# Three more pairs by seven products, ten stages' diagonal tiles on ScalarE, and a new order of steps

## The chip, the cores and the metric

The kernel runs on one core of a Trainium2 chip. Its time is the device time of one execution in microseconds (us), as the median of several runs. Five engines work side by side, each with its own queue in order: TensorE (PE, with its weight loads shown as PEld), VectorE (DVE), ScalarE (ACT), GpSimd (POOL) and SyncE (SP), which here only issues transfers.

## The reference

Two operations follow each other: a recurrent attention with a decaying state, and a two-layer network with a leaky activation.

```python
batch, n_heads, seq, head_dim = (4, 8, 768, 48)
for t in range(S):
    cur = np.einsum('bhd,bhe->bhde', u[None] * kt, vt)
    y[:, :, t] = np.einsum('bhd,bhde->bhe', rt, state + cur)
    state = w[None, :, :, None] * state + np.einsum('bhd,bhe->bhde', kt, vt)
...
n_tokens, d_model, d_ff = (3072, 384, 2048)
h = x @ w_in
g = np.maximum(0.01 * h, h)
return (g @ w_out).astype(np.float32)
```

The inputs are float32, the output is float32 of 3072 x 384.

## The kernel before

**Stages and pairs.** The 4 x 768 tokens are cut into 24 stages of 128 tokens, numbered n = 0 to 23; six stages make one sequence, so stages 0, 6, 12 and 18 start from an empty state. Two stages make a pair, m = 0 to 11, and the network works on pairs. The work of the attention inside a stage is done in chunk form: scaled queries and keys, a 128 x 128 product per head, a mask, and a state that is carried to the next stage.

**The list of steps.** The order of all work is one string, ORDER (L25 to L27). Each word is a step with its stage or pair; the program goes through the words, and each step appends its instructions to the queues of the engines it uses. Nothing is reordered afterwards, so the list sets the order in every queue at once. An instruction waits, by semaphores that `Sched.resolve` finds, for whatever wrote its inputs or still reads its target. The words:

- k, r, v and a number: load that stage's keys, queries or values by a transfer that POOL issues; wi and wo load a quarter of the weights each, also by POOL. Keys and queries lie in 14 buffers.
- P: scale queries and keys (VectorE, one instruction, or two where the word has no ".1" and n < 4). For n >= 8 the step also lets SP issue a transposing transfer, qk to tp.
- T: for n < 8 the transpose by TensorE, with two evictions on ScalarE. X: for n < 6 a product on VectorE for the diagonal.
- A: the 128 x 128 products of a stage, in two PSUM banks. M: mask and evict them into the tile `at` (VectorE).
- K: products of keys and values for the state. S: the state's update (VectorE).
- Q: for n < 6 one product on VectorE; for later stages three VectorE instructions that give `s_tok`, one number per token and head, and then `diag_tile` (L351), which fills `at` with a diagonal matrix for each head. M later writes the masked products over it, leaving the diagonal.
- Y: the output of the attention, with an eviction to xT on ScalarE.
- G (a stage, a quarter of the first layer) and J (a pair, an eighth of it): products into one bank, with the activation on ScalarE into gT.
- H (a stage): the second layer, 16 products of 384 columns, an eviction on ScalarE, and a store that SP issues.
- V, B and Z: the second layer of a pair by seven products of half size in place of eight. V (four steps, once) forms sums of weight blocks in `tw`, B (four steps a pair) sums of blocks of gT in `gs`, both on VectorE. Z (seven steps a pair) has 8 products of 192 columns each; ScalarE copies a partial sum to `snap`, or VectorE adds one, and the finished half of a row block is stored.
- U, C, W: small tables. F: filler products without a result. I: skip so many PSUM banks.

Every step that needs a bank takes the next of eight in turn (`next_bank`), so a step waits for the reader of the step that had the bank before; I lets the turn pass banks that a Z sequence still holds.

**Before the change** Z is used for the pairs 8 to 11 and H for the stages 0 to 15. All diagonal tiles of stages 6 to 23 are made by POOL, two instructions of 128 x 512 each, in the queue that also issues all loads. In `g2_seven`, `store` writes out a row block of 128 x 384 when its second half has landed; the last pair alone stores each half by itself.

## Time and profile before

| | |
|---|---|
| median of 3 runs | 169.43 us (169.15 to 169.71) |
| the profiled execution | 169.63 us, span 167.8 us |
| granted TensorE clock, mean | 1.00 |
| instructions | 5041 |
| loads and stores in HBM | 20.45 MB read, 4.72 MB written |

The span is the part of an execution that the trace covers, from its first to its last event. In the rows of the trace "PE" is the product, "PEld" its weight load; "L561" is the line of the kernel; out<-in names the tiles. A row of a group has its count, the busy time, the mean of one in ns, the idle time of the engine just before, and what ended it. A row of the timeline starts with the start and the length in us. A row of the stretches has the stretch, its length, the busy time of each engine with its count of instructions, the granted clock, the transfer engines' share and GB/s.

### The profile page before, as it was taken

To read this page: it belongs to the slowest core of one execution; us is meant where nothing else is said; L and a number is where in the kernel's file an instruction comes from. 1 tells how busy PE (TensorE), PEld (TensorE's weight loads), DVE (VectorE), ACT (ScalarE), POOL (GpSimd) and SP (SyncE) were. 2 spreads that over 40 slices of the span, in tenths; PEclk is the share of its full clock that TensorE was granted. 3 is DMA by queue.
4 is the path that set the end of the run, shared out by engine and by line. 5 is a ranking of instruction groups with operands and counts; after the bars stand their busy time and mean duration, and the time that the engine had idled before them with its cause. 6 is when DMAs were issued, how large, how long until landed. Compare 5 with 4: busy or idle time off the path is not lost.

```text
span 167.8 us, 5041 instructions
## 1 busy us (share of the span) xinstructions
PE 159.4 (95%) x2166; PEld 126.3 (75%) x2166; DVE 117.8 (70%) x205; ACT 94.2 (56%) x179; POOL 107.0 (64%) x119
## 2 busy tenths in 40 slices
PE   6697899999999999999899999999999999999993
PEld 2265698898566769955778887766699889999992
DVE  7399987927605979989898499935899396313571
ACT  4766678798223448821549783521288787485310
POOL 7999999999999899797999963750044200000000
PEclk9999999999999999999999999999999999999999
DMA  5999999999999999999999997512125000110224
GB/s 99 120 132 144 170 180 164 184 205 149 148 159 198 168 142 149 223 132 132 169 145 132 108 141 120 117 47 95 49 71 108 0 4 0 47 51 0 78 69 141
DMA packets 100090, 19.67 MB, mean 117 GB/s; under 512 B 93154, under 2 KB 100068, under 8 KB 100068
## 3 DMA queue, kind: packets, MB, share of 16 engines
q0 software_dynamic: 76512, 10.03, 95.5%
q1 hardware_dynamic: 22514, 9.12, 27.2%
q8 instruction: 17, 0.28, 0.7%
q10 hardware_dynamic: 1042, 0.20, 0.6%
q14 instruction: 5, 0.04, 0.1%
HBM read 20.45 MB, written 4.72 MB: 150 GB/s over the span
## 4 chain that ended last, share of the span: by engine, by line
PE 81%; DMA 9%; POOL 7%; issue 1%; DVE 0%; ACT 0%; POOLq 0%; DVEq 0%; ACTq 0%
PE ps_all L561 32%; PE ps_all L578 22%; PE ps_all L650 11%; PE ps_all L544 6%; POOL rk_sb L213 5%; DMA tp<-qk 5%; PE ps_all L511 4%; DMA w_in_sb<-in_moe_w_in_dram 4%; PE ps_all L388 3%; POOL v_sb L213 2%; PE ps_all L438 2%; PE ps_all L368 1%; PE ps_all L516 0%; POOL w_in_sb L228 0%; DVE at L398 0%
## 5 line engine op out<-in xcount | busy, mean ns | idle before, releaser
L561 PE MATMUL ps_all<-xT,w_in_sb 128*128 128x256 bf16 x480 | 57.0, 273 | 0.0
L567 ACT ACTIVATE gT<-ps_all 128x512 bf16<-128x512 f32 x80 | 47.8, 597 | 12.9 <-PE ps_all L561 9.3
L355 POOL TENSOR_TENSOR at<-ident,s_tok 128x512 bf16<-128x512 bf16 x36 | 39.3, 1119 | 23.0 <-DVE s_tok L347 22.9
L561 PEld LDWEIGHTS ps_all<-xT,w_in_sb 128*128 128x128 bf16 x480 | 45.8, 98 | 6.1
L578 PE MATMUL ps_all<-w_out_sb,gT 128*128 128x384 bf16 x256 | 43.5, 326 | 0.0
L578 PEld LDWEIGHTS ps_all<-w_out_sb,gT 128*128 128x128 bf16 x256 | 24.5, 98 | 15.8
L398 DVE CAST_PREDICATED at<-mask,ps_all 128x1024 bf16<-128x1024 uint16 x18 | 21.4, 1218 | 15.3 <-PE ps_all L388 15.2
L584 ACT ACTIVATE out_sb<-ps_all 128x384 f32<-128x384 f32 x16 | 7.9, 491 | 37.0 <-PE ps_all L578 37.0
L213 POOL DMA_DIRECT2D v_sb<-in_v_dram x24 | 22.5, 942 | 0.3 <-issue 0.3
L213 POOL DMA_DIRECT2D rk_sb<-in_k_dram x23 | 21.2, 929 | 0.0
L213 POOL DMA_DIRECT2D rk_sb<-in_r_dram x23 | 21.0, 923 | 0.0
L313 DVE TENSOR_TENSOR qk<-rk_sb,tab 128x768 bf16<-128x768 bf16 x23 | 16.0, 704 | 4.4 <-DMA rk_sb<-in_r_dram 4.4
L544 PE MATMUL ps_all<-xT,w_in_sb 128*128 128x128 bf16 x192 | 12.7, 219 | 0.8 <-DMA w_in_sb<-in_moe_w_in_dram 0.8
L481 DVE TENSOR_TENSOR sum_t<-ps_all,st 128x384 bf16<-128x384 f32 x14 | 7.7, 552 | 6.4 <-PE ps_all L438 6.3
L544 PEld LDWEIGHTS ps_all<-xT,w_in_sb 128*128 128x128 bf16 x192 | 11.1, 98 | 1.3 <-DVE prod L328 0.9
L345 DVE TENSOR_TENSOR ku<-rk_sb,ku 128x384 bf16<-128x384 bf16 x18 | 11.3, 628 | 0.6
L531 ACT ACTIVATE xT<-ps_all 128x384 bf16<-128x384 f32 x24 | 10.5, 493 | 2.1 <-PE ps_all L516 1.4
L549 ACT ACTIVATE gT<-ps_all 128x512 bf16<-128x512 f32 x16 | 9.6, 603 | 3.7 <-PE ps_all L544 3.4
L511 PE MATMUL ps_all<-at,v_sb 128*32 128x128 bf16 x384 | 10.5, 220 | 0.1
L347 DVE TENSOR_REDUCE s_tok<-ku 128x8 f32<-128x384 bf16 x18 | 9.9, 553 | 0.6
L375 ACT ACTIVATE tp<-ps_all 128x512 bf16<-128x512 f32 x16 | 8.7, 600 | 2.9 <-PE ps_all L368 2.9
L616 DVE TENSOR_TENSOR gs<-gT 128x1024 bf16<-128x1024 bf16 x8 | 5.4, 687 | 7.0 <-PE ps_all L650 5.3
(75 smaller groups left out, 188.3 us busy)
## 6 DMA issues: line engine op xcount, KB each, us to landing
out_dram<-out_sb SPq DMA_DIRECT2D x22, 192.0 KB, 2.6
v_sb<-in_v_dram POOLq DMA_DIRECT2D x24, 96.0 KB, 6.5
rk_sb<-in_k_dram POOLq DMA_DIRECT2D x23, 96.0 KB, 6.4
rk_sb<-in_r_dram POOLq DMA_DIRECT2D x23, 96.0 KB, 7.0
w_in_sb<-in_moe_w_in_dram POOLq DMA_DIRECT2D x4, 384.0 KB, 7.5
w_out_sb<-in_moe_w_out_dram POOLq DMA_DIRECT2D x4, 384.0 KB, 8.5
out_dram<-out_sb SPq DMA_DIRECT2D x4, 96.0 KB, 1.6
tp<-qk SPq DMA_TRANSPOSE x16, 4.4
```

Source lines behind the costliest of these rows:

```text
L213: add("pool", lambda: G.dma_start(dst, src), R=pace, W=[key], dma=f"{which}{n}")
L313: add("dve", lambda: V.tensor_tensor(qk[iq][:, :, 0:D], both, by, ALU.mult), R=[("r", n % NRK), ("k", n % NRK), "qtab", "ktab", ("qk0", iq ...
L345: add("dve", lambda: V.tensor_tensor(ku[i2][:, :], r_of(n), ku[i2][:, :], ALU.mult), R=[("r", n % NRK), ("ku", i2)], W=[("ku", i2), ("rku" ...
L355: add("pool", lambda hh=hh, s_of=s_of: G.tensor_tensor(at[ia][:, hh, :, :], ident[:, :].unsqueeze(1).to_broadcast([128, NP, 128]), s_of.un ...
L398: add("dve", lambda: V.copy_predicated(at[n % NAT][:, :, :, :].rearrange("p two m i -> p (two m) i"), mask[:, :].bitcast(mybir.dt.uint16). ...
L511: last = PE.matmul(ps_y[32 * q:32 * q + 32, 128 * s:128 * s + 128], a, m, start=first_mm and (s == 0 or n >= DIAG), stop=last_mm and n >= ...
L531: add("act", lambda: A.activation(xT[m % NX][:, :, 128 * half:128 * half + 128], ps_y[:, 0:HD].rearrange("p (s t) -> p s t", t=128), AF.Copy),
L544: last = PE.matmul(ps_g[:, 128 * f:128 * f + 128], w_in_sb[:, s, 128 * fb:128 * fb + 128], xT[ix][:, s, t], start=s == 0, stop=s == NSL - 1)
L561: last = PE.matmul(ps_g[:, 256 * f:256 * f + 256], w_in_sb[:, s, 128 * fb:128 * fb + 128], xT[ix][:, s, :], start=s == 0, stop=s == NSL - 1)
L567: add("act", lambda: A.activation(gT[ig][:, 2 * j:2 * j + 2, :].rearrange("p f t -> p (f t)"), ps_g[:, :], AF.Prelu, alpha=0.01), R=[key], ...
L578: last = PE.matmul(ps_o[:, 0:HD], gT[ig][:, s, 128 * half:128 * half + 128], w_out_sb[:, s, :], start=s == 0, stop=s == NFB - 1)
L650: done = PE.matmul(ps_o[:, 0:NH], lhs[:, s, :], rhs[:, s, :], start=first and s == 0, stop=s == HF - 1, skip_group_check=not (first and last))
```

## The change

Four edits. The list ORDER is replaced by another one with the same kinds of step (466 words in place of 434). The diagonal tiles of stages 14 to 23 are made by ScalarE, eight instructions of 128 x 128 a stage, one for each head, with that head's column of s_tok as the scale. Pairs 5, 6 and 7 join the pairs with seven products, so that H is left for the stages 0 to 9. The last two pairs store each half of a row block by itself, where only the last one did. The lists, cut to their beginnings and to a part further on that the prediction speaks of:

```diff
-v0 U k1 k2 I1 P0 r1 P1.1 r2 k3 T0 F4 C W A0 r3 X0 P2.1 wi3 T1 K0 M0.0 Q0 T2 X1 S0 P3.1 Y0 X2 A2 M2.4 T3 v1 K1 G0.3 k4 Q1 A1 r4 A3 S1 P4 v2 K2 M1.2 T4 v3 k5 Y1 X3 Q2 M3.0 wi2 S2 K3 Y2 Q3 G1.3 G1.2
...
+P0 k1 r1 I4 k3 T0 k2 r3 r2 I1 r4 P1.0 v0 I3 X0 T1 W k4 v1 U P3.1 wi3 k5 P2.1 F2 I3 A1 X1 C T3 v2 M1.0 r5 v3 wi1 P4 v4 v5 r9 I2 K0 Q0 T2 X3 A0 T4 S0 K1 M0.4 r6 k6 I4 I4 Q1 wi0 A2 A3 S1 M2.1 X2 Y1 M3.2 P5 I1 Y0 G1.3 K2 r7 k7 v6 k9 wi2 wo0 wo3 S2 G0.3 v7 K3 T5 Q2 Q3 A4 S3 wo1 wo2 X4 X5 M4.0 Y2 Y3 G1.1
...
+k14 A7 r10 G0.2 J2.2 M7 J2.4 K7 J2.5 S7 G2.2 V0 Y6 Y7 Q8 J2.0 P8 J2.6 P9 r16 r23 I4 H3 H1 H0 P11 r21 Q11 J3.0 Q10 P10 J3.5 P13 J3.4 J3.3 H2 r15 K8 k12 v12 A8 A9 J3.2 M9 r12 J3.6 M8 k16 k15 S8 H4 K9 v11 Y9 I3 Q13 v18 k19 k17 v14 S9 Y8 J3.1 K10 P14 J4.0 S10 J4.5 J4.2 J4.6 J3.7 k18 v21 r17 k21 v13 Q14 P12 r18 J4.1 A11 A10 M11 I1 Q15 Q12 J4.7 H5 H7 M10 Y11
...
+Z6.0 J7.6 Z6.1 Z6.2 Q20 B6.3 Q21 Z6.3 K19 Z6.4 P23 J8.7 J8.0 J8.3 P21 I1 Z6.5 S19 J7.2 Z6.6 A20 J8.6 J7.4
...
```

```diff
-    SEVEN = (8, 9, 10, 11)
+    AT = (14, 15, 16, 17, 18, 19, 20, 21, 22, 23,)
+    SEVEN = (5, 6, 7, 8, 9, 10, 11)
...
     def diag_tile(n, i2):
         ia = n % NAT
+        if n in AT:
+            for h in range(H):
+                add("act", lambda h=h: A.activation(at[ia][:, h % 2, h // 2, :], ident[:, :], AF.Copy,
+                                                    scale=s_tok[i2][:, h:h + 1]),
+                    R=["ident", ("s", i2)], W=[("at", ia, h % 2)])
+            return
         for hh in range(2):
...
-            if final:
+            if m >= NST // 2 - 2:
                 add("sp", lambda: SP.dma_start(out[128 * n:128 * n + 128, cols], out_sb[io][:, cols]),
                     R=[("o", io, c)], W=[("out", n, c)], dma=f"o{io}{c}")
```

## The prediction

> **What bounds the kernel now.** I read first the page's busy shares, then the busy time by stretches of the span, then the chain that ended last, and only then groups and single instructions. The page names TensorE; the stretches (stretch, its length, then busy time of PE, PEld, DVE, ACT, POOL) say since when:

> ```profile
> PE 159.4 (95%) x2166; PEld 126.3 (75%) x2166; DVE 117.8 (70%) x205; ACT 94.2 (56%) x179; POOL 107.0 (64%) x119
> 6.40:22.00 15.60, 13.70 (x234) 10.17 (x235) 12.52 (x27) 9.90 (x22) 15.60 (x19) 1.00 2.11 148
> 35.00:74.00 39.00, 39.00 (x431) 28.98 (x431) 26.96 (x41) 20.71 (x38) 37.55 (x41) 1.00 1.92 170
> 74.00:83.00 9.00, 8.47 (x180) 5.78 (x178) 8.00 (x13) 3.12 (x7) 7.94 (x10) 1.00 1.67 130
> 83.00:100.00 17.00, 17.00 (x217) 14.20 (x211) 13.77 (x20) 11.77 (x21) 15.53 (x17) 1.00 2.10 136
> 100.00:165.00 65.00, 65.00 (x829) 54.50 (x827) 42.35 (x70) 33.85 (x67) 12.37 (x11) 1.00 0.25 58
> 165.00:167.80 2.80, 0.00 (x1) 0.00 (x0) 0.00 (x0) 0.33 (x1) 0.00 (x0) 1.00 0.49 171
> ```

> From 35 us to 165 us TensorE is busy all the time but for 0.53 us. So only three things move the end: the amount of TensorE work, the idle time before about 22 us (1.9 us after the first transposes, and products that wait on loads), and the 2.8 us after the last product. Any gain on another engine is worth nothing by itself; any new wait of TensorE costs its full length.

> The chain (start, length, work) gives what a step costs when nothing holds it:

> ```profile
> 13.59 7.27 DMA w_in_sb<-in_moe_w_in_dram
> 23.27 0.45 PE ps_all L368 x8
> 30.53 1.34 PE ps_all L544 x24
> 54.48 0.17 PE ps_all L438 x4
> 59.22 0.90 PE ps_all L511 x56
> 64.95 3.93 PE ps_all L561 x36
> 74.95 7.60 DMA tp<-qk
> 85.38 2.60 PE ps_all L578 x16
> 93.46 0.33 PE ps_all L388 x8
> 152.46 12.55 PE ps_all L650 x152
> ```

> T 0.45, G 0.67 (24 products are two), K 0.17, Y 0.45 (56 are two), J 0.655 (36 are six), H 2.60, A 0.33; one of the seven products Z has 8 instructions, 12.55 / 19 = 0.66.

> **The products.** A pair by two H steps takes 5.20 us of TensorE, by seven Z steps 7 x 0.66 = 4.62. Pairs 5, 6 and 7 change over: 3 x 0.58 = **1.73 us less**. It is a full gain, since these pairs lie where TensorE never stops. What they add elsewhere, by these rows:

> ```profile
> L584 ACT ACTIVATE out_sb<-ps_all 128x384 f32<-128x384 f32 x16 | 7.9, 491 | 37.0 <-PE ps_all L578 37.0
> L398 DVE CAST_PREDICATED at<-mask,ps_all 128x1024 bf16<-128x1024 uint16 x18 | 21.4, 1218 | 15.3 <-PE ps_all L388 15.2
> L658 ACT ACTIVATE snap<-ps_all 128x192 f32<-128x192 f32 x12 | 4.0, 331 | 4.9 <-PE ps_all L650 4.6
> L616 DVE TENSOR_TENSOR gs<-gT 128x1024 bf16<-128x1024 bf16 x8 | 5.4, 687 | 7.0 <-PE ps_all L650 5.3
> L681 DVE TENSOR_TENSOR out_sb<-ps_all,snap 128x192 f32<-128x192 f32 x13 | 4.6, 357 | 5.5 <-PE ps_all L650 5.5
> ```

> VectorE gets four sums and three additions a pair, 4 x 0.687 + 3 x 0.357 = 3.8 us, 11.5 for three; ScalarE four copies of 0.331 for two of 0.491, 1.0 us in all. Hidden while the engines keep up with TensorE. The four V steps move ahead by some forty steps; their work stays the same.

> **The diagonal tiles.** For ten stages POOL loses two instructions of 1.119 us, 22.4 us in all, and ScalarE gets eight of 128 columns with a scale column. No such instruction is in the trace. The nearest are these two, with a scale column and a source in SBUF, and the one behind them:

> ```profile
> L355 POOL TENSOR_TENSOR at<-ident,s_tok 128x512 bf16<-128x512 bf16 x36 | 39.3, 1119 | 23.0 <-DVE s_tok L347 22.9
> 5.11 0.61 ACT L295 ACTIVATE tab<-lnw,qexp 128x384 bf16<-128x384 f32 x1
> 5.63 0.60 ACT L296 ACTIVATE tab<-lnw,kexp 128x384 bf16<-128x384 f32 x1
> 83.65 2.08 POOL L355 TENSOR_TENSOR at<-ident,s_tok 128x512 bf16<-128x512 bf16 x2
> 83.65 2.29 DVE L345 TENSOR_TENSOR ku<-rk_sb,ku 128x384 bf16<-128x384 bf16 x1
> 77.05 0.36 DVE L345 TENSOR_TENSOR ku<-rk_sb,ku 128x384 bf16<-128x384 bf16 x1
> ```

> They start 0.52 apart for 384 columns. From 192 to 384 columns a copy goes from 331 to 491 ns, 0.83 ns a column; 256 columns fewer take 0.21 off, so 0.31 each, between 0.31 and 0.39 (0.60 less 0.21, no overlap). I take 0.31, as eight stand in a row: 2.45 us a stage, 24.5 us for ten. ScalarE goes from 94.2 to 119.7 us, 72% of the span.

> The last three rows show what POOL's tiles cost today: VectorE's product of 0.36 us takes 2.29 while POOL multiplies. That gives some of the 11.5 us back; how much does not matter, because VectorE does not set the end after 35 us.

> What can matter is order. The new ScalarE instructions stand in its queue ahead of the evictions that free TensorE's eight banks, and the first of each eight waits for VectorE's s_tok. At its tightest, Q20 and Q21 stand together: 4.9 us, then J8.7's eviction of 0.5. Until the list takes J8.7's bank again TensorE has Z6.3, K19, Z6.4, J8.7, J8.0, J8.3, Z6.5, J7.2, Z6.6, A20, J8.6: 4 x 0.66 + 0.17 + 5 x 0.655 + 0.33 = 6.4 us. That covers it by 1.0 us, if VectorE has s_tok in time. Behind Q14, J4.1's eviction is done after 2.45 + 0.5 us and its bank is wanted after J4.1, A11, A10, J4.7 and H5, 3 x 0.66 + 2.6 = 4.6.

> **The start.** The page rows for loads and the rows that set the start:

> ```profile
> rk_sb<-in_r_dram POOLq DMA_DIRECT2D x23, 96.0 KB, 7.0
> 4.14 1.78 POOL L213 DMA_DIRECT2D rk_sb<-in_r_dram  x2
> 8.57 0.56 DVE L313 TENSOR_TENSOR qk<-rk_sb,tab 128x768 bf16<-128x768 bf16 x1 [1.72 <-DMA rk_sb<-in_r_dram]
> 13.59 0.83 POOL L228 DMA_DIRECT2D w_in_sb<-in_moe_w_in_dram  x1
> 19.86 0.54 DVE L338 TENSOR_TENSOR vs<-v_sb,ps_all 128x384 bf16<-128x384 bf16 x1
> 20.99 1.50 PE L544 MATMUL ps_all<-xT,w_in_sb 128*128 128x128 bf16 x24 [0.75 <-DMA w_in_sb<-in_moe_w_in_dram]
> 82.69 0.62 PE L388 MATMUL ps_all<-tp 48*128 48x128 bf16 x16 [0.53 <-DMA tp<-qk]
> ```

> Today stage 1's r is the fourth load, issued at 4.14, and VectorE gets it at 8.57, 4.4 us later. In the new list it is the second, issued near 2.4, so P1 starts near 6.9. From there to Q3 (which ended at 20.4) VectorE gets P5 ahead, P1 in two halves, and waits for the loads of stages 3, 2 and 0 (fifth, sixth, eighth, so 9.5, 10.4 and 12 to 13). Its old 11.8 us become about 13.2 plus 1.5 of waits: Q3 ends near 21.6 and Y3 near 22.2. The next step, G1.1, also needs wi1, now the sixteenth load. In the old list fourteen loads lie between 1.35 and wi2's issue at 13.59, 0.874 each; fifteen give 14.5, and with wi2's 7.27 it lands at 21.7. I take 22.5 for G1.1, between 21.7 and 23.5. By then the new list has done one T, one A and one Y more than the old one at 20.99 (1.23 us). So 22.5 - 20.99 - 1.23 = **0.3 us lost**, between 0.5 gained and 1.3 lost.

> **The middle.** After that the list has no idle time if every load and tile comes in time. POOL issues a load every 0.89 us or so; k8 stands behind 36 loads and three diagonal stages (2.18 us each): 1.35 + 32.0 + 6.5 = 39.9, landing near 46.5. The list wants it on VectorE when TensorE has done 26 us of its work, at 15 + 26 = 41. VectorE stands for some 5 us, again for r10, and comes out at S8 near 59.2, while Y9, which needs that state, is due at 59.7. TensorE's cover in between is J2.6, H3, H1, H0, four J3 and H2, over 13 us. A landing 1 us later than that is a stall. The trace bounds such a place from below by nothing and shows one of 0.53 us (the transposes row). With places like it at stages 8, 10, 12 and 19 I take **0.9 us**, between 0 and 3.

> **The end.** Pair 10 now stores halves, so the last transfer is half a row block instead of a whole one:

> ```profile
> out_dram<-out_sb SPq DMA_DIRECT2D x22, 192.0 KB, 2.6
> out_dram<-out_sb SPq DMA_DIRECT2D x4, 96.0 KB, 1.6
> 165.10 0.33 ACT L674 ACTIVATE out_sb<-ps_all 128x192 f32<-128x192 f32 x1 [3.69 <-PE ps_all L650]
> ```

> After the last copy ended at 165.43 the span still had 2.37 us. The halves land 1.0 us sooner: I take **0.8 us gained**, between 0 and 1.0. Two more stores on SP stand behind no transpose.

> **Sum.** -1.73 + 0.3 + 0.9 - 0.8 = -1.33 us. The profiled execution took 169.63 (span 167.8 and 1.83 around it) and would take 168.3; the runs' median is 0.2 lower, so 168.1.

> **A rule against it.** In the start eight transposes take the longer time below at first, the shorter later, at a granted clock that the profile gives as 1.00 throughout:

> ```profile
> 9.69 1.03 PE L368 MATMUL ps_all<-ident,qk 128*128 128x128 bf16 x8
> 13.29 0.62 PE L368 MATMUL ps_all<-ident,qk 128*128 128x128 bf16 x8
> ```

> The change takes two of four filler products out of the start (0.43 each) and puts K0 ahead of T2, so TensorE stands until v0 lands. If the slow speed then lasts until 22 us, the steps T2, A0, T4, K1, A2, A3 and two G cost their 3.4 us once more, of which about half lies under VectorE: 1.7 us. [...]

> **The rivals.**
> - *No wait in the middle.* For it: from 35 to 165 us the old list has one stall of 0.53. Against: VectorE's waits for k8 and r10. 169.43 - 1.73 + 0.3 - 0.8 = 167.2; with the start at its best 166.4. I say 166.9.
> - *Loads late.* POOL's queue sets k8, r10, r12; each landing 1 us later at the first two is a us of TensorE, 2.1 instead of 0.9: 169.3, no change.
> - *ScalarE's queue (slower).* VectorE may reach Q14 and Q21 late. Its list work in excess of TensorE's, summed step by step (M 1.22, Q some 1.26, P 0.55 and the rest by their rows), has grown to 4.2 us at the first and 3.2 at the second. ScalarE then stands too, with the evictions behind it: 4.2 + 2.45 + 0.5 - 4.6 = 2.5 and 3.2 + 4.9 + 0.5 - 6.4 = 2.2. With 4.7 in the middle: 171.9. It decides once the middle costs over 2.2 us. For it: VectorE, ScalarE and the banks now stand in series. Against: VectorE waited 15.2 us for A in the old list, so it was seldom in arrears.
> - *A cold start (slower)*, as above: 168.1 + 1.7 = 169.8, with a later wi1 170.3.

> **Chances.** Forecast 0.46 (its own range 167.3 to 168.9), no wait 0.12, loads 0.14, ScalarE's queue 0.19, cold start 0.09. About 0.3%, 0.5 us, is what a measurement of this kernel can tell from no change. Faster 0.46 + 0.12 = 0.58, within 0.14, slower 0.28. The range 166.6 to 171.6 cuts the lowest corner of the no-wait case and ScalarE's at its full price.

> **What would show it.** Right: TensorE's products at L578 fall by 96 and those of the sevens rise by 168; its busy time falls by near 1.7; the first G1.1 near 22.5; under 1.5 us of idle between 23 us and the end; under 2 us after the last copy. ScalarE's new tiles: about 0.31 us apart. Wrong: idle of TensorE whose releaser is ScalarE's eviction or VectorE's s_tok near 66 or 110 us (the third rival), VectorE waiting on k or r for longer than 6 us near 41 us with TensorE idle at Y9 (the second), transposes near 1 us for eight after 14 us (the fourth).

## The result, and the profile after

The changed kernel took 173.74 us (median of four runs, 172.97 to 174.45) beside 169.50 for the kernel before on the same chip: 1.025 times as long, 95% interval 1.020 to 1.030. In a later set on another chip it took 172.91 (171.60 to 173.69), 1.019 times as long (1.015 to 1.024). The forecast was 168.1 us. The profiled execution took 174.45, its span 172.6; it was the longest of its four, so its trace shows somewhat more loss than the medians do.

The busy shares on the page of the changed kernel, and its row of the granted clock in 40 slices of 4.3 us:

```profile
PE 161.1 (93%) x2236; PEld 132.1 (77%) x2236; DVE 122.9 (71%) x228; ACT 116.7 (68%) x265; POOL 85.3 (49%) x99
PEclk9999969999999999999999999999999999999999
```

TensorE's busy time went up by 1.7 us where 1.7 less was forecast, though it now has less to do. The clock row gives a first reason: a slice behind 21 us ran at 0.6. The rest shows in the busy time by stretches, the first row that of the kernel before, the others those of the changed one:

```profile
0.00:35.00 35.00, 29.97 (x525) 22.79 (x526) 26.74 (x64) 24.42 (x47) 33.65 (x44) 1.00 1.85 151
```

```profile
0.00:35.00 35.00, 29.00 (x471) 21.68 (x472) 25.20 (x63) 22.56 (x44) 29.10 (x39) 0.95 1.88 151
35.00:65.00 30.00, 29.99 (x377) 22.62 (x376) 22.50 (x33) 16.07 (x31) 29.11 (x31) 1.00 1.62 143
65.00:100.00 35.00, 32.03 (x400) 24.23 (x398) 27.87 (x48) 28.68 (x73) 27.06 (x31) 1.00 2.11 154
100.00:160.00 60.00, 60.00 (x876) 53.78 (x875) 40.65 (x74) 45.76 (x112) 0.00 (x0) 1.00 0.27 62
```

From these rows the span splits without a remainder. Take TensorE's busy time of the whole span less that of the first 35 us, and call it the work left at 35 us: 159.4 - 29.97 = 129.43 before, 161.1 - 29.00 = 132.10 after. Add the 35 us, TensorE's idle time from 35 to 160 us, and what remains, which lies at the end.

| us | before | after | difference |
|---|---|---|---|
| work left at 35 us | 129.43 | 132.10 | +2.67 |
| idle from 35 to 160 us | 0.53 | 2.97 | +2.44 |
| the end | 2.84 | 2.53 | -0.31 |
| span, with the 35 us | 167.8 | 172.6 | +4.8 |

By the forecast the new program has 1.73 us less work in pairs 5 to 7, all of it behind 35 us. At equal progress it would have had 127.70 left; it had 132.10. So the first 35 us lost **4.4 us**, the stretch from 65 to 100 us lost **2.4**, the products and the end gave back 1.73 and 0.31.

**Where the first 35 us went.** A row of VectorE and the products that follow (start, length, idle time in brackets with what ended it), then the two stretches behind them:

```profile
19.88 1.01 DVE L339 TENSOR_TENSOR vs<-v_sb,ps_all 128x384 bf16<-128x384 bf16 x2
21.10 0.27 PE L518 MATMUL ps_all<-at,v_sb 128*32 128x128 bf16 x4
23.24 0.27 PE L518 MATMUL ps_all<-tp,st 128*32 128x128 bf16 x1 [1.87 <-issue]
25.38 2.56 PE L551 MATMUL ps_all<-xT,w_in_sb 128*128 128x128 bf16 x36
```

```profile
22.00:25.00 3.00, 1.76 (x45) 1.25 (x44) 1.62 (x4) 0.49 (x1) 3.00 (x5) 0.63 1.89 177
25.00:30.00 5.00, 5.00 (x103) 4.71 (x99) 1.12 (x3) 3.29 (x6) 4.41 (x6) 0.88 2.01 172
```

VectorE was done with Q2 and Q3 at 20.9, a little ahead of the 21.6 forecast. But in the middle of the step Y2 TensorE stood for 1.87 us, and the row names no engine and no transfer: "issue" is a wait for nothing that the profile shows. Behind it the clock was 0.63 and 0.88, by single microseconds 0.50 from 23 to 26: three products of L523 took 0.50 us at 25.09, beside 0.34 at 17.38, and G1.1 began at 25.38 instead of 22.5.

**Where the middle went.** The rows of VectorE, POOL and TensorE that hang together, in order of time, the last a piece of the chain of waits:

```profile
28.25 0.56 DVE L339 TENSOR_TENSOR vs<-v_sb,ps_all 128x384 bf16<-128x384 bf16 x1 [4.62 <-PE ps_all L445]
34.40 4.17 POOL L362 TENSOR_TENSOR at<-ident,s_tok 128x512 bf16<-128x512 bf16 x4 [4.99 <-DVE s_tok L348]
43.20 1.83 POOL L214 DMA_DIRECT2D rk_sb<-in_k_dram  x2
74.11 2.77 PE L585 MATMUL ps_all<-w_out_sb,gT 128*128 128x384 bf16 x16 [0.55 <-ACT gT L574]
86.46 0.62 PE L395 MATMUL ps_all<-tp 48*128 48x128 bf16 x16 [1.25 <-DMA tp<-qk]
92.37 0.52 PE L445 MATMUL ps_all<-v_sb,qk 128*128 128x96 bf16 x8 [1.08 <-DMA v_sb<-in_v_dram]
96.13 0.56 DVE L314 TENSOR_TENSOR qk<-rk_sb,tab 128x768 bf16<-128x768 bf16 x1 [2.96 <-DMA rk_sb<-in_r_dram]
```

```profile
85.86 10.18 DMA rk_sb<-in_r_dram
```

They are to be read from above. K4 was late by the start's loss, so VectorE waited 4.62 us for it; VectorE's s_tok for stage 6 was late with it, and POOL stood 4.99 us at the diagonal tiles of stages 6 and 7. All further loads are behind these in POOL's queue: k8 was issued at 43.20. TensorE itself did not stand between 35 and 65 us (29.99 of 30.00 busy). It stood at 74 us for an eviction, and at 86 and 92 us for a transposed tile and for v15; VectorE stood at 96 for r19, issued at 85.86 and landed 10.18 us later.

**The tiles and the products**, by groups (count, then busy time, mean of one in ns, idle time ahead):

```profile
L356 ACT ACTIVATE at<-ident,s_tok 128x128 bf16<-128x128 bf16 x80 | 24.3, 388 | 3.4 <-DVE s_tok L348 3.2
L585 PE MATMUL ps_all<-w_out_sb,gT 128*128 128x384 bf16 x160 | 27.3, 326 | 0.5 <-ACT gT L574 0.5
```

```profile
71.14 2.45 ACT L356 ACTIVATE at<-ident,s_tok 128x128 bf16<-128x128 bf16 x8 [1.50 <-DVE s_tok L348]
```

Eight tiles take 2.45 us, 0.31 apart, and all 80 take 24.3. The line is not on the chain of waits. H has 160 products in place of 256.

**The end.** The last copy, and the stores of the two pairs with halves (kilobytes, us from issue to landing):

```profile
170.17 0.33 ACT L681 ACTIVATE out_sb<-ps_all 128x192 f32<-128x192 f32 x1 [3.69 <-PE ps_all L657]
out_dram<-out_sb SPq DMA_DIRECT2D x8, 96.0 KB, 1.6
```

After the last copy the span had 172.6 - 170.5 = 2.1 us, before 2.37.

### The profile page after: what moved, and what is told of

Same layout as the page of the kernel before. It is cut to its first block, busy times and chain, and to the rows that moved or that the text cites. A ratio compares the mean times of both kernels' runs of the same rounds, so it can differ in the third digit from the quotient of the medians.

```text
span 172.6 us, 5276 instructions
## 1 busy us (share of the span) xinstructions
PE 161.1 (93%) x2236; PEld 132.1 (77%) x2236; DVE 122.9 (71%) x228; ACT 116.7 (68%) x265; POOL 85.3 (49%) x99
## 4 chain that ended last, share of the span: by engine, by line
PE 53%; POOL 24%; DMA 13%; DVE 5%; issue 3%; POOLq 1%; ACT 0%; DVEq 0%; ACTq 0%
PE ps_all L657 19%; PE ps_all L568 17%; DMA rk_sb<-in_r_dram 13%; POOL rk_sb L214 11%; POOL at L362 8%; POOL v_sb L214 6%; PE ps_all L518 4%; PE ps_all L551 3%; PE ps_all L395 3%; PE ps_all L375 2%; PE ps_all L585 2%; PE ps_all L445 1%; DVE sum_t L488 1%; PE ps_all L523 1%; DVE ku L346 1%
## 5 line engine op out<-in xcount | busy, mean ns | idle before, releaser
L568 PE MATMUL ps_all<-xT,w_in_sb 128*128 128x256 bf16 x480 | 59.2, 273 | 0.0
L574 ACT ACTIVATE gT<-ps_all 128x512 bf16<-128x512 f32 x80 | 46.8, 594 | 15.0 <-PE ps_all L568 12.7
L585 PE MATMUL ps_all<-w_out_sb,gT 128*128 128x384 bf16 x160 | 27.3, 326 | 0.5 <-ACT gT L574 0.5
L356 ACT ACTIVATE at<-ident,s_tok 128x128 bf16<-128x128 bf16 x80 | 24.3, 388 | 3.4 <-DVE s_tok L348 3.2
L585 PEld LDWEIGHTS ps_all<-w_out_sb,gT 128*128 128x128 bf16 x160 | 15.5, 98 | 10.4 <-ACT gT L574 0.9
L214 POOL DMA_DIRECT2D v_sb<-in_v_dram x24 | 22.4, 953 | 0.0
L214 POOL DMA_DIRECT2D rk_sb<-in_k_dram x23 | 21.4, 942 | 0.3 <-issue 0.3
L362 POOL TENSOR_TENSOR at<-ident,s_tok 128x512 bf16<-128x512 bf16 x16 | 17.6, 1141 | 5.9 <-DVE s_tok L348 5.9
L314 DVE TENSOR_TENSOR qk<-rk_sb,tab 128x768 bf16<-128x768 bf16 x22 | 15.2, 704 | 4.0 <-DMA rk_sb<-in_r_dram 4.0
L657 PE MATMUL ps_all<-tw,gs 128*128 128x192 bf16 x168 | 16.3, 246 | 0.0
L657 PEld LDWEIGHTS ps_all<-tw,gs 128*128 128x128 bf16 x168 | 14.2, 98 | 0.2
L518 PE MATMUL ps_all<-tp,st 128*32 128x128 bf16 x240 | 10.3, 227 | 1.9 <-issue 1.9
L518 PEld LDWEIGHTS ps_all<-at,v_sb 128*32 128x32 bf16 x384 | 8.5, 98 | 4.5 <-issue 3.4
L344 DVE TENSOR_TENSOR ku<-rk_sb,u_tab 128x384 bf16<-128x384 bf16 x18 | 9.0, 500 | 3.7 <-DMA rk_sb<-in_k_dram 3.7
## 6 DMA issues: line engine op xcount, KB each, us to landing
out_dram<-out_sb SPq DMA_DIRECT2D x20, 192.0 KB, 3.4
```

The source lines that it names most:

```text
L214: add("pool", lambda: G.dma_start(dst, src), R=pace, W=[key], dma=f"{which}{n}")
L314: add("dve", lambda: V.tensor_tensor(qk[iq][:, :, 0:D], both, by, ALU.mult), R=[("r", n % NRK), ("k", n % NRK), "qtab", "ktab", ("qk0", iq ...
L356: add("act", lambda h=h: A.activation(at[ia][:, h % 2, h // 2, :], ident[:, :], AF.Copy, scale=s_tok[i2][:, h:h + 1]), R=["ident", ("s", i ...
L362: add("pool", lambda hh=hh, s_of=s_of: G.tensor_tensor(at[ia][:, hh, :, :], ident[:, :].unsqueeze(1).to_broadcast([128, NP, 128]), s_of.un ...
L518: last = PE.matmul(ps_y[32 * q:32 * q + 32, 128 * s:128 * s + 128], a, m, start=first_mm and (s == 0 or n >= DIAG), stop=last_mm and n >= ...
L568: last = PE.matmul(ps_g[:, 256 * f:256 * f + 256], w_in_sb[:, s, 128 * fb:128 * fb + 128], xT[ix][:, s, :], start=s == 0, stop=s == NSL - 1)
```

## The experiments

Kernels of one set ran on one chip, beside the kernel before, and each ratio is to that kernel in the same set. Ratios are compared across sets, medians only within one. "Left" and "idle" are the two terms of the table above, worked out in the same way from each kernel's own rows.

| label | start | loads | median us (runs) | ratio, 95% | left | idle |
|---|---|---|---|---|---|---|
| e8_after_again | new | new | 172.91 (6) | 1.019, 1.015 to 1.024 | 131.25 | 1.59 |
| e2_loads_first | new | five moved ahead | 170.94 (10) | 1.007, 1.004 to 1.010 | 130.82 | 0.51 |
| e10_after_sorted | new | sorted | 170.13 (12) | 0.999, 0.995 to 1.003 | 130.99 | 0.00 |
| e15_after_sorted_again | new | sorted | 170.22 (8) | 1.006, 1.003 to 1.009 | 130.21 | 0.55 |
| e1_old_start | old | new | 169.51 (10) | 0.998, 0.994 to 1.002 | 131.29 | 2.04 |
| e6_sorted | old | sorted | 168.00 (12) | 0.990, 0.987 to 0.992 | 128.56 | 0.00 |
| e12_sorted_again | old | sorted | 168.85 (6) | 0.988, 0.982 to 0.994 | 129.68 | 0.00 |
| e16_sorted_third | old | sorted | 168.37 (11) | 0.992, 0.989 to 0.996 | 130.76 | 0.00 |
| e14_old_start_no_filler | old, no fillers | sorted | 167.61 (7) | 0.989, 0.985 to 0.994 | 128.66 | 0.73 |

Some profiled executions were long ones: e1's took 172.69 us, the longest of its ten, e16's 170.12 and e14's 168.71. Their last two numbers are those of long runs, and one program's work left differs by up to 2.2 us between executions (e6, e12 and e16).

### The changed kernel again

No edit. It measures how far one program's runs lie apart.

> The changed kernel itself, once more, so that the other runs of this set have it on the same chip. In every trace so far TensorE stopped for something no semaphore explains after its 219th product, at 346 and at 472, whatever the list had there. If it is the supply of TensorE's instructions, in blocks of 127 products, the stop is again right after the 219th product, in Y2, of another length than 1.9 us. If it was chance it is gone. Time 172.5 to 174.

172.91 us, span 170.4 in the profiled one. The stop in Y2 was there again with 1.09 us in place of 1.87, the mean clock was 1.00 in place of 0.99, and POOL stood 2.78 us at stage 6 in place of 4.99. So the place of the stop belongs to the program; its length and the clock belong to the run, and the wait of POOL follows them.

### Loads ahead of the waiting instruction

e2 moves five loads in front of Q6, whose tiles POOL waits for; nothing else differs from the changed kernel.

```diff
-... P7 G1.0 Q6 G2.0 Q7 Y5 T7 G0.0 I1 r8 G3.0 A6 J2.3 k13 r14 J2.7 M6 Q9 k8 G1.2 K6 G3.2 k11 v9 r11 ...
+... P7 G1.0 r8 k13 r14 k8 k11 Q6 G2.0 Q7 Y5 T7 G0.0 I1 G3.0 A6 J2.3 J2.7 M6 Q9 G1.2 K6 G3.2 v9 r11 ...
```

> The changed kernel with five load words (r8 k13 r14 k8 k11) moved ahead of Q6, so that POOL issues them in the 5 us in which it stood at Q6. The start is left as it is. The chain theory: the loads behind them come 4 to 5 us earlier, TensorE's idle time between 65 and 98 us falls from 3.0 to under 1 us, the time to 171 to 172 us. The rival, that loads and transposes collide in the middle because POOL issues them without pause, sees the idle time stay near 3 us and the time near 173.7.

e10 puts all loads behind Y4 in the order in which the list first uses them, six of them ahead of Q6, where the changed kernel has one. The first words show the principle:

```diff
-... K5 r13 G2.1 S4 Q5 T6 P7 G1.0 Q6 G2.0 Q7 Y5 ... r8 G3.0 A6 J2.3 k13 r14 J2.7 M6 Q9 k8 G1.2 K6 G3.2 k11 v9 r11 v8 J2.1 v10 k10 S6 k14 A7 r10 ... P9 r16 r23 I4 H3 H1 H0 P11 r21 Q11 ...
+... K5 r8 G2.1 S4 Q5 T6 P7 G1.0 k8 k11 r11 k10 r10 Q6 G2.0 Q7 Y5 ... G3.0 A6 J2.3 J2.7 M6 Q9 G1.2 K6 G3.2 r13 k13 v8 J2.1 v9 v10 S6 r14 A7 k14 ... P9 k12 r12 I4 H3 H1 H0 P11 r15 Q11 ...
```

> The changed kernel with its own start, its loads behind Y4 sorted by first use and five of them ahead of Q6. Theory: the rest of the list then has no idle time, as with the old start, and what is left is the price of the new start. Idle from 35 to 160 us under 0.5 us; 170.3 to 171.2, and 2.3 to 3 us behind the old start with sorted loads in the same set. Rival: the new start costs little by itself, its loss lies in the loads that come late: then under 169.5.

e2 gave 170.94, ratio 1.007 against 1.019 to 1.025 for the changed kernel, and e10 170.13, ratio 0.999: the order of the loads alone brings the changed kernel back to the time of before, or within 0.6% of it in the second set (e15, 1.006). POOL's queue and TensorE's stretches in e10:

```profile
28.38 1.05 POOL L214 DMA_DIRECT2D rk_sb<-in_r_dram  x1
29.25 1.92 POOL L214 DMA_DIRECT2D rk_sb<-in_k_dram  x2
33.61 4.25 POOL L362 TENSOR_TENSOR at<-ident,s_tok 128x512 bf16<-128x512 bf16 x4
```

```profile
0.00:35.00 35.00, 27.81 (x480) 20.54 (x481) 26.23 (x64) 23.19 (x45) 34.09 (x45) 1.00 1.86 149
35.00:160.00 125.00, 125.00 (x1690) 104.32 (x1686) 95.88 (x156) 92.06 (x218) 51.14 (x55) 1.00 1.10 109
```

The tiles of stage 6 now find s_tok ready, since POOL comes to them with the loads ahead of them already issued; k8 goes out at 29.25 instead of 43.20, and TensorE has no idle time from 35 to 160 us. The theory of the middle holds. By the ratios the order of the loads was worth 1.019 - 0.999 = 2.0%, 3.4 us, or 1.019 - 1.006 = 1.3%, 2.2 us, with the second set of the same sorted kernel; in the traces left and idle together fall by 1.8 us from e8 and by 4.1 from the first execution of the changed kernel.

### The old start

e1 takes the old list's words up to G3.0 and then the new list's remaining ones. The single words "I1" between them let the turn pass banks, nothing more.

```diff
-P0 k1 r1 I4 k3 T0 k2 r3 r2 I1 r4 P1.0 v0 I3 X0 T1 W k4 v1 U P3.1 wi3 ... T7 G0.0 I1 r8 G3.0 A6 J2.3 k13 r14 J2.7 M6 Q9 k8 ...
+v0 U k1 k2 I1 P0 r1 P1.1 r2 k3 T0 F4 C W A0 r3 X0 P2.1 wi3 T1 K0 ... P7 G3.2 k8 r8 T7 G3.0 r13 I1 G1.0 I1 G2.0 Q7 J2.3 k13 r14 I1 J2.7 Q9 K6 ...
```

> The changed kernel with the old list's words up to G3.0 and the new list's remaining words after them, so that the first 32 us of the kernel before stand in front of the new middle and end. The chain theory says that the start costs twice: TensorE loses some 3.5 us by itself near 21 to 26 us, and because K4 is late, s_tok of stage 6 is late, POOL stands 5 us at Q6 with all loads behind it, and the loads of stages 15 and 19 come too late near 86 to 96 us. With the old start both go: POOL's wait before its first diagonal tile under 1 us, TensorE's idle time from 35 us to the end under 1 us, a time near 168 us. The rival, that the new middle places loads and transposes too close whatever the start, keeps 2 to 3 us idle between 65 and 98 us and gives 170 to 171 us.

It took 169.51 us, as long as before (0.998). In the set of e2 that is 1.4 us less than with the loads mended and the new start kept. But the middle did not go with it, as the row of TensorE's K15 in the profiled execution shows:

```profile
90.82 0.51 PE L445 MATMUL ps_all<-v_sb,qk 128*128 128x96 bf16 x8 [1.37 <-DMA v_sb<-in_v_dram]
```

The idle time from 35 us on was still 2.04 us. POOL waited 1.96 us, for the tiles of stage 7. So the loads stand late in the new list by themselves, not only because the start delays POOL. e6 therefore keeps the old start and sorts the loads behind it by first use, four of them ahead of Q7, where e1 has one:

```diff
-... T7 G3.0 r13 I1 G1.0 I1 G2.0 Q7 J2.3 k13 r14 I1 J2.7 Q9 K6 k11 v9 r11 v8 I1 J2.1 v10 k10 S6 k14 A7 r10 ...
+... T7 G3.0 r11 k10 r10 k11 I1 G1.0 I1 G2.0 Q7 J2.3 I1 J2.7 Q9 K6 r13 k13 v8 I1 J2.1 v9 v10 S6 r14 A7 k14 ...
```

> The old start with the new middle (the run with the old list's words up to G3.0), and the loads behind G3.0 put in order of their first use, three of them ahead of Q7 where POOL stood 2.0 us. If the middle's idle time (2.0 us between 65 and 100 us in that run) is late loads, it falls below 0.6 us and the time by about 1.5 us against that run, to 168 to 168.5, faster than the kernel before. The rival, transposes that collide with unpaced loads, keeps over 1 us of idle time behind tp.

> The old start with sorted loads once more, for a second set of times beside the other three: 167.8 to 168.4, no idle time of TensorE from 35 to 160 us.

> The old start with sorted loads a third time, as the measure for its start without fillers: 167.8 to 168.8.

168.00, 168.85 and 168.37 us in three sets, 0.8 to 1.2% faster than before in each. The stretches of e6:

```profile
0.00:35.00 35.00, 28.84 (x526) 21.88 (x527) 28.65 (x66) 24.27 (x47) 34.09 (x45) 1.00 1.87 153
35.00:160.00 125.00, 125.00 (x1675) 104.45 (x1673) 94.95 (x155) 91.14 (x218) 50.98 (x56) 1.00 1.09 108
```

This is the version that beats both kernels, together with e14 below. With sorted loads the old start is 170.13 - 168.85 = 1.3 us better than the new one in one set and 170.22 - 168.37 = 1.9 in another.

**The sort alone.** e9 sorts the loads of the kernel before in the same way and changes nothing else.

```diff
-... T7 G3.0 k18 Q7 K6 v10 r12 J2.3 r20 k13 J2.7 v8 r13 r11 S6 k10 J2.2 v20 k11 K7 ...
+... T7 G3.0 v8 k13 r13 v9 Q7 K6 J2.3 r11 J2.7 k11 r12 k12 S6 k10 J2.2 r10 k14 K7 ...
```

> The kernel before with nothing changed but the order of its loads behind k8: each load stands in the order in which the list first uses it, and three stand ahead of Q7. If the 168.0 us of the old start with sorted loads came from the sort alone, this one should gain as much: 168.0 to 168.5. If the sort only takes idle time away, there is 0.53 us of it in the old list from 35 us on, so 169.2 to 169.8 against 169.7 for before. I expect the second.

170.04 us, ratio 0.998 (0.994 to 1.002): no gain. The old list had only 0.53 us of idle time to lose there. The 1% of e6 therefore comes from the rest of the change, which pays once its loads come in time.

### The tiles on ScalarE

e3 leaves the changed list as it is and gives all tiles back to POOL.

```diff
-    AT = (14, 15, 16, 17, 18, 19, 20, 21, 22, 23,)
+    AT = ()
```

> The changed kernel with all diagonal tiles on POOL, list and pairs as changed. If POOL's freed time makes loads bunch and collide with transposes, the middle's idle time falls below 1.5 us and the time to 172 us or less. If the loads are late because POOL reaches them late, four more pairs of tiles ahead of r19 (2.2 us each) make it worse: 175 us or more. Its first 60 us hold the same instructions as the changed kernel, so it also shows whether TensorE's stop of 1.9 us in the middle of Y2 near 21 us and the low granted clock behind it come back: a property of the list says both within 0.5 us, chance says not.

178.48 us (178.20 to 178.62), ratio 1.051, about 5 us more than the changed kernel. TensorE was idle 6.10 us from 35 to 160. A row of VectorE shows what the new list asks of POOL:

```profile
82.97 1.22 DVE L405 CAST_PREDICATED at<-mask,ps_all 128x1024 bf16<-128x1024 uint16 x1 [2.67 <-POOL at L362]
```

e4 does the reverse: the old list with its four pairs of sevens, with the tiles of stages 14 to 23 on ScalarE and the halves stored.

```diff
 v0 U k1 k2 I1 P0 r1 P1.1 r2 k3 T0 F4 ...
+    AT = (14, 15, 16, 17, 18, 19, 20, 21, 22, 23,)
     SEVEN = (8, 9, 10, 11)
```

> The kernel before with its own list and four pairs of sevens, and the diagonal tiles of stages 14 to 23 on ScalarE and the half stores of the last two pairs added. If ScalarE's queue is the cost (tiles ahead of evictions), TensorE gets new idle time behind ScalarE and the time rises by 1 us or more, to 170.5 or above. If the tiles are hidden, the time stays within 0.6 us of the kernel before, 168.9 to 169.8, with 0.3 us less at the end from the half stores.

175.86 us, ratio 1.036 (1.028 to 1.044). It lost 5.8 us, the first of the two cases that were expected, and far above the 1 us named there. The first and the last piece of the six of ScalarE's tiles on its chain of waits, and the longest stop of TensorE:

```profile
81.09 2.45 ACT at L356 x8
...
135.94 2.31 ACT at L356 x8
```

```profile
98.50 2.79 PE L568 MATMUL ps_all<-xT,w_in_sb 128*128 128x256 bf16 x24 [2.56 <-ACT xT L538]
```

Here the prediction's third rival is real: eight tiles stand in ScalarE's queue ahead of an eviction to xT, and the first layer waits for it. So the tiles are worth 5 us on the new list and, with the half stores, cost 6 on the old one.

### The seven products

e7 puts pairs 5 to 7 of the changed kernel back on H, each pair's two H steps in the places of its Z3 and Z6, without B. e11 does the same to e6.

```diff
-    SEVEN = (5, 6, 7, 8, 9, 10, 11)
+    SEVEN = (8, 9, 10, 11)
...
-B5.0 H8 B5.2 V2 K16 J6.4 B5.1 Y15 S16 Y14 A16 M16 P20 Z5.0 J7.0 Z5.1 J7.5 B5.3 Z5.2 Y17 Y18 Y16 V3 Q23 Z5.3
+H8 V2 K16 J6.4 Y15 S16 Y14 A16 M16 P20 J7.0 J7.5 Y17 Y18 Y16 V3 Q23 H10
```

> The changed kernel with the pairs 5, 6 and 7 back on H (the list's B and Z words of these pairs taken out, H10 to H15 in place of their fourth and seventh Z). The sum's first term says 1.73 us more than the changed kernel, less what its stalls in the middle hide; a rise of 1 to 2 us supports it. If the sevens cost more on VectorE than they save on TensorE, the time falls.

> The old start with sorted loads, pairs 5 to 7 by H instead of seven products. TensorE has no idle time there that could hide the difference, so the term of 1.73 us should show in full: 1.4 to 1.9 us longer than the kernel with sevens in the same set (169.4 to 169.9). If the sevens' additions on VectorE and ScalarE or their tails on TensorE eat part of it, under 1.2 us.

e7 took 173.88 beside 172.91, 1.0 us more; e11 170.90 beside 168.85, 2.05 us more. TensorE's busy time, first e7 and e8, then e11 and e12:

```profile
PE 161.2 (94%) x2164; PEld 126.6 (74%) x2164; DVE 113.1 (66%) x207; ACT 115.5 (67%) x259; POOL 85.3 (50%) x99
```

```profile
PE 159.3 (93%) x2236; PEld 130.9 (77%) x2236; DVE 122.3 (72%) x228; ACT 116.7 (68%) x265; POOL 85.3 (50%) x99
```

```profile
PE 159.6 (93%) x2166; PEld 125.4 (73%) x2166; DVE 114.4 (67%) x205; ACT 114.9 (67%) x259; POOL 85.1 (50%) x99
```

```profile
PE 157.7 (94%) x2238; PEld 129.7 (78%) x2238; DVE 126.1 (75%) x226; ACT 115.7 (69%) x265; POOL 85.3 (51%) x99
```

1.9 us in both pairs, where 1.73 was forecast. One program's busy time itself differs between executions, by 1.2 us from e6 to e16 (157.4 and 158.6), so two single traces cannot show the difference that closely. On the changed list part of the gain is lost in waits; with sorted loads it shows in full.

### The stop without a releaser

The stop in Y2 came after 218 of TensorE's products in every trace of the new start. The old start with the new middle has one too, after 219 products, in the middle of G1.3, in all but e14 and e18. Further ones followed after the 345th and the 471st or 472nd, 126 or 127 apart. e5 puts 24 products of two columns, without a result, ahead of T0; everything behind keeps its order.

```diff
-P0 k1 r1 I4 k3 T0 k2 r3 ...
+P0 k1 r1 I4 k3 E24 T0 k2 r3 ...
...
+            for _ in range(n):
+                last = PE.matmul(ps[i][:, 0:2], ones[:, 0:128], ones[:, 0:2], start=True, stop=True)
```

> The changed kernel with 24 products of two columns, without a result, put ahead of T0, where TensorE waits 1.9 us anyway. The supply theory says that the stop follows the count and not the step: it moves to the 195th product of the list, at the border of T5 and A4, and the next to the 322nd. The length may change, as TensorE gets there earlier or later than the block. The rival, that Y2 waits for something of its own (a state, a tile), keeps the stop in Y2. The time should stay within 1.5 us of the changed kernel; no theory gives its sign.

```profile
27.01 0.90 PE L561 MATMUL ps_all<-xT,w_in_sb 128*128 128x128 bf16 x13 [1.08 <-issue]
32.99 0.23 PE L528 MATMUL ps_all<-tp,st 128*32 128x128 bf16 x1 [0.92 <-issue]
```

It took 172.20 us beside 172.91. Y2 ran through. The first border, 219 products with the 24 new ones, now fell at the end of T5, near 20.9 us; the packet told of below had started at 16.90, 4.0 us ahead, and TensorE did not stop. The next stops came in a step of G and in Y5, after the 345th and 472nd product with the 24 counted, so 24 of the old products earlier. The stop goes by the count of instructions, not by the step. 127 products with their weight loads are 254 instructions.

The page has a row for what brings them. Here it is for the changed kernel (packets, megabytes, share of the 16 transfer engines), and below it the same row for the stretch from 20.75 to 21.00 us:

```profile
q8 instruction: 17, 0.28, 0.6%
```

```profile
q8 instruction: 1, 0.02, 24.4%
```

17 packets of 0.28 / 17 = 0.0165 MB for TensorE's 4,472 products and weight loads, one for every 263, and as many for the 4,332 of the kernel before. The author's reading of these counts is that the queue fetches TensorE's program in blocks. One packet takes 24.4% of 16 engines for 0.25 us, 0.98 us of one engine. With the stretch narrowed to 0.05 us, the packet's start can be set beside the time when TensorE went on, that is, began the first product behind the border:

| kernel | packet starts | TensorE goes on | later by | stop before it |
|---|---|---|---|---|
| after | 20.75 | 23.24 | 2.49 | 1.87 |
| e8_after_again | 19.85 | 22.28 | 2.43 | 1.09 |
| e15_after_sorted_again | 19.60 | 22.12 | 2.52 | 0.18 |
| e12_sorted_again | 18.55 | 20.80 | 2.25 | 0.70 |
| e16_sorted_third | 19.70 | 22.04 | 2.34 | 1.91 |
| e5_tiny, second border | 24.70 | 27.01 | 2.31 | 1.08 |
| e9_before_sorted | 18.55 | 21.23 | 2.68 | 1.26 |
| before | 17.70 | 19.96 | 2.26 | none |

There were 38 such stops of 0.18 us or more in 17 of the traces. For 37 of them the third number lay between 2.24 and 2.68 us, while the stops themselves were 0.18 to 1.93 us long. For the other, in e11, it was 2.97 us, and its packet took 1.47 us of an engine (36.8% of 16 engines for 0.25 us). A stop without a releaser is not always of this kind: in e3 one of 1.91 us ended at 84.77, 6.8 us behind the last packet. The reading that fits these times: TensorE goes on when its next block has come, 2.24 to 2.68 us after the packet starts in 37 of the 38; if it has used up the block ahead of that, it stands. The kernel before and e9 have the same first 219 products and the same loads up to there, and only e9 stopped:

```profile
19.36 0.88 PE L544 MATMUL ps_all<-xT,w_in_sb 128*128 128x128 bf16 x12
21.23 1.62 PE L544 MATMUL ps_all<-xT,w_in_sb 128*128 128x128 bf16 x26 [1.26 <-issue]
```

The first row is that of the kernel before. The border lies behind the tenth of its twelve products; the eleventh began at 19.96, 2.26 us after the packet's start, without a stop, and what TensorE waited for at 20.99 was put down to w_in. So whether the old start stops, and for how long, belongs to the execution. In the profiled execution of the kernel before all the waits listed for TensorE have a releaser; that of the changed one has the stop of 1.87 us, and that of e9 the one of 1.26.

### What else the new start costs

With sorted loads 1.3 to 1.9 us remained between the two starts. TensorE's transposes of the changed kernel were slow for longer than in the old start, and the row at 13.75 is the last slow one:

```profile
13.75 1.03 PE L375 MATMUL ps_all<-ident,qk 128*128 128x128 bf16 x8
```

In e16 the same eight took 0.62 from 9.49 us on. e13 moves the filler products of e10 to the front and makes them four; e14 takes them out of e6.

```diff
-P0 k1 r1 I4 k3 T0 k2 r3 r2 I1 r4 P1.0 v0 I3 X0 T1 W k4 v1 U P3.1 wi3 k5 P2.1 F2 I3 A1 ...
+P0 k1 r1 I4 k3 T0 F4 k2 r3 r2 I1 r4 P1.0 v0 I3 X0 T1 W k4 v1 U P3.1 wi3 k5 P2.1 I3 A1 ...
```

```diff
-v0 U k1 k2 I1 P0 r1 P1.1 r2 k3 T0 F4 C W A0 ...
+v0 U k1 k2 I1 P0 r1 P1.1 r2 k3 T0 C W A0 ...
```

> The changed kernel with sorted loads, and in its start four filler products right behind T0 in place of two behind P2.1. Theory: what is left of the new start's price is TensorE's slow pace, which lasted there to about 15.4 us (eight transposes 1.03 us at 13.75) and in the old start to 9.6 or 12 us; four fillers without a gap bring the fast pace earlier. Then eight transposes take 0.62 us from about 11 us on, and the time falls by 1 to 2 us against the changed kernel with sorted loads, to within 0.5 us of the old start with sorted loads. Rival: the pace is hidden behind VectorE and loads, the time stays within 0.5 us, and the price of the start is in the order of its steps.

> The old start with sorted loads, its four filler products taken out. Theory: TensorE is slow until about 15 us (eight transposes 1.0 us at 13 us) as in the new start, and the time rises by 1 to 2 us to 169.5 to 170.8. Rival: TensorE is 1.9 us ahead without the fillers and the slow pace is hidden: 168 to 168.8.

> The changed kernel with sorted loads once more, as the measure for the early fillers: 169.8 to 170.4, eight transposes 1.0 us up to 13.8 us.

The transposes of e13, and then those of e14:

```profile
12.63 1.05 PE L375 MATMUL ps_all<-ident,qk 128*128 128x128 bf16 x8
14.16 0.68 PE L375 MATMUL ps_all<-ident,qk 128*128 128x128 bf16 x8
```

```profile
13.61 1.03 PE L375 MATMUL ps_all<-ident,qk 128*128 128x128 bf16 x8
```

The fillers did not bring the fast pace forward: it came at 14.2 us, and in e15 at 13.2. So e13 (169.50, 0.7 us under e15) says nothing of the pace, and its gain is unexplained. e14 asks from the other side: without fillers the old start is as slow as the new one up to 14 us, and at 167.61 us it is no slower than with them (168.37). The 1 to 2 us that the theory asked for did not come. e14's trace had no stop without a releaser either, as its first packet started at 17.75; a smaller cost of the slow pace, made up for by the missing stop, is not excluded.

Two last kernels asked whether loads delay the packets. e17 moves five weight loads of 384 KB, and r9 and k9, of e10 behind the loads of stages 8, 10 and 11, and wi0 three loads later. e18 moves wi1 and wi0 of e14 ahead to wi2.

```diff
-... I4 I4 Q1 wi0 A2 ... Y0 G1.3 K2 r7 k7 v6 k9 wi2 wo0 wo3 S2 G0.3 v7 ... A4 S3 wo1 wo2 X4 ... G1.0 k8 k11 r11 k10 r10 Q6 ...
+... I4 I4 Q1 A2 ... Y0 G1.3 K2 r7 k7 v6 wi0 S2 G0.3 v7 ... A4 S3 X4 ... G1.0 k8 k11 r11 k10 r10 r9 k9 wi2 wo0 wo3 wo1 wo2 Q6 ...
```

```diff
-... Q2 M3.0 wi2 S2 K3 Y2 Q3 G1.3 G1.2 r5 r6 k6 v4 wi1 G2.2 v5 r7 wi0 v6 ...
+... Q2 M3.0 wi2 wi1 wi0 S2 K3 Y2 Q3 G1.3 G1.2 r5 r6 k6 v4 G2.2 v5 r7 v6 ...
```

> The changed kernel with sorted loads, and in its start five weight loads of 384 KB (wi2, wo0 to wo3) and the loads r9 and k9 moved behind the loads of stages 8, 10 and 11, and wi0 three loads later. In all traces so far TensorE goes on 2.2 to 2.7 us after the start of a 16.5 KB packet in the queue called instruction, whatever the length of its stop. Theory: that packet starts late where the transfer engines are full of loads, so with 2 MB less asked for up to 28 us the second and third packet (25.6 to 26.2 and 31.3 to 32.0 us) start 0.5 to 2 us earlier, the stops after the 346th and 472nd product (0.4 and 0.5 to 0.8 us) shrink, and the time falls by 0.5 to 1.5 us from 170.2 to 168.7 to 169.7. The first packet hardly moves, since wi0 alone of these lies near it. Rival: the packet's time goes by TensorE's own progress, the stops stay, 169.9 to 170.5.

> The old start without fillers and with sorted loads (167.6 us, its first packet of instructions at 17.75 us, no stop of TensorE without a named releaser), and the loads wi1 and wi0 moved ahead to wi2, so that 768 KB more are asked for ahead of 17 us. Theory: the first packet starts at 19 to 21 us, TensorE stops after its 219th product and goes on 2.2 to 2.7 us behind the packet, at 21.3 to 23.5, and the time rises by 1 to 2.5 us, to 168.6 to 170. Rival: the packet stays near 17.8 us; what rises is waits on loads r5 to v4 alone, under 1 us.

Their longest waits of TensorE behind 20 us, e17 and then e18:

```profile
38.73 0.83 PE L551 MATMUL ps_all<-xT,w_in_sb 128*128 128x128 bf16 x12 [3.03 <-DMA w_in_sb<-in_moe_w_in_dram]
```

```profile
25.02 0.62 PE L375 MATMUL ps_all<-ident,qk 128*128 128x128 bf16 x8 [2.03 <-DVE qk L314]
```

Both were slower, 171.51 and 170.56 us, each with a new wait for a load that now came late (in e18 VectorE's product qk waited for r). For the question itself they disagree. In e17 the third packet started at 30.55 instead of 31.3 to 32.0 and the stop after the 471st product was gone, as the theory said; the second packet hardly moved (25.50), and the stop behind it was 0.10 us, as in e15. In e18 the first packet started at 16.35, earlier than the 17.75 of e14 and not later: here more data asked for ahead of it did not delay it. What sets the time of a packet stays open.

## Why the prediction was wrong, step by step

- **The products** were right. The forecast was 1.73 us; TensorE's busy time fell by 1.9 in both comparisons, each a difference of two single traces, and the time by 2.05 where no wait hid it.
- **The diagonal tiles** were right for this list: 0.31 us each, 24.3 us in all, not on the chain. They are also needed: with them on POOL the list takes 5 us longer. The bound by the banks held but for 0.55 us at 74.11, where H waits for the eviction that stands behind the tiles at 71.14.
- **The start** was the step that failed most in the profiled execution: "between 0.5 gained and 1.3 lost", and 4.4 us were lost by 35 us. It summed loads, VectorE's work and semaphores, and that part was near the edge of its bounds: in e15, with a stop of only 0.18 us, G1.1 began at 23.41 (forecast 21.7 to 23.5), and 23.41 - 20.99 - 1.23 = 1.2 us lost. By the reading of the packets, it put at nothing that TensorE's own program has to arrive. The stop of 1.87 us agrees with that; the clock of 0.50 from 23 to 26 us and the later G1.1 came behind it. But such stops are no mark of the new start alone: e9 and the old start of e1, e6, e12 and e16 have them, and it was luck that the one trace behind the forecast had none. An estimate separates the two. With the stops without a releaser ahead of 35 us taken off the work left (for e10 130.99 less 1.42, 0.38 and 0.82), five traces of the new start (e2, e8, e10, e13, e15) keep 128.4 to 129.4 us and four of the old one (e1, e6, e12, e14) 127.3 to 128.7, beside 127.70 at equal progress. So the order of the steps cost about 1 us, within the bounds, and the stops came on top, 0.8 to 2.6 us in those five traces and 0 to 3.0 in those four. By the medians with sorted loads the new start costs 1.3 to 1.9 us.
- **The middle** fell into its range at the wrong place, which is luck. 2.44 us lie in the range of 0 to 3, and are nearly three times the 0.9 taken; by the medians the order of the loads cost 2.2 to 3.4. The step took POOL to issue a load every 0.89 us without a stop and so had k8 out at 39.9. POOL stood 4.99 us at stage 6, k8 went out at 43.20, and what TensorE lacked in the end were stage 15's transposed tile (1.25 us) and v15 (1.08), not Y9's state. The failing line is "POOL issues a load every 0.89 us or so": it names what POOL issues, and not the instruction in the same queue that waits for VectorE. e2 and e10 show it, since with loads put ahead of that instruction the idle time falls to 0.51 and 0.00. e1 adds that the list's order of loads was late in itself, which the prediction did not compare with the order of first use.
- **The end** was too large: 0.31 us for 0.8. The halves land after 1.6 us as forecast, but the last of the stores is only one part of the 2.1 us that remain.
- **The rivals.** "No wait in the middle" was wrong on the changed list and right once its loads were sorted (0.00 in e10). "Loads late" named the right queue, but with its price at stages 8 and 10, where VectorE's waits came to 5.6 us and TensorE did not stand. "ScalarE's queue" was wrong here (0.55 us of its 2.5) and right for the old list with the same tiles (e4). "A cold start" had its sign right, slow transposes up to 13.75 us. All that is shown of its rule is the pace of its two rows, 1.03 and 0.62 us for eight transposes. That the slow pace lasts until 22 us and costs 1.7 us was the author's estimate, and no run shows it: eight transposes of the changed kernel took 0.61 us at 20.10, and e14, still at 1.03 us at 13.61, took 167.61 us beside 168.37 with the fillers.

## What to carry to other kernels

Follow each in-order queue that issues loads up to the first instruction in it that waits for another engine, and put the loads that are due next ahead of it, in the order of their first use; a moved start then costs its own delay once and not again at every late load. In a long unrolled program look also at the transfers that bring the instructions: here TensorE stood 38 times in 17 traces, 0.18 to 1.93 us each, at places that went by the count of instructions. An edit that moves work to another engine is judged together with the order that it was made for: the same ten stages of tiles on ScalarE were worth 5 us on one list and cost 6, with the half stores, on the other.
